# Cumulative log sums as two float32r products from the sixth unit on, with routing weights finished a step later

## The chip, the cores and the metric

The kernel runs on one core of a Trainium2 chip. A core has a matrix engine (TensorE, PE in the profile; its weight loads are listed as PEld), a vector engine (VectorE, DVE), a scalar engine (ScalarE, ACT), a general engine (GpSimd, POOL) and a sync engine (SyncE, SP) that mostly issues transfers. The engines run their own instruction streams in order and wait for each other through semaphores. Sixteen DMA engines move data between memory and the on-chip buffer. Matrix products are written to PSUM, which has eight banks here.

The metric is the time of one execution on the device in microseconds (us); lower is better. The figure used is the median over several executions.

## The reference, cut to what matters

The first half is a gated linear recurrence over 768 time steps, for 4 batches and 8 heads of width 48. The second half is a two-level mixture of experts on the 3072 resulting rows.

```python
f = 1 / (1 + exp(-f_logit))
for t in range(S):
    state = f[:, :, t, :, None] * state + outer(k[:, :, t], v[:, :, t])
    y[:, :, t] = q[:, :, t] @ state
x = y.transpose(0, 2, 1, 3).reshape(3072, 384)
g_idx = argmax(x @ w_group);  e_idx = argmax(x @ w_expert[g_idx])
weight = softmax(group)[g_idx] * softmax(expert)[e_idx]
out = weight * (relu(x @ w1[g, e]) @ w2[g, e])     # one expert of 16 for each row
```

## The kernel before

**Units.** The recurrence is computed in chunks of 128 time steps. A unit is one chunk of two batches, so there are 12 units, numbered 0 to 11 (`NU` is 12): unit 2c is the first half of the batches of chunk c, unit 2c+1 the second half. A product of gates over a chunk is an exponential of a sum of logs. So a unit's gate logits are clamped (L581, `bounded`, VectorE), turned into the negative logs nl = log(1 + exp(-f)) by an Exp and a Ln on ScalarE (L591 and L594, `gated`, 128x768 elements each), and summed along time by a product with a triangular matrix of ones (L600, tile `cs`, one 128x384 float32 product for each of the unit's two batches). Two exponentials of each sum (L601, L602) scale q and k (L620, L623, `multiplied`). Then come transposes of q and k (L634) and their copies to SBUF (L635), the scores (L659, `ap`) and their triangular mask on VectorE (L662, `am`), the state (L676 `ds` on TensorE, then L682 and L683 on VectorE, the second of which needs `decays`, a transpose of the last row of each chunk, L643 and L644), the outputs (L697 from the state, L701 from the masked scores, copied by L704), the logits of the router (L717, L722, reduced by L723) and the rows turned back and copied out (L742 to L747).

**Routing.** When both units of a chunk have their logits, `route` runs for the chunk as a generator that is advanced by one step for every `r` in the order. Its steps on VectorE are: the differences to the maximum and a first mark (L187 to L191); the choice (L194 to L198); counts on TensorE and an Exp of the differences on ScalarE (L203 to L206); the position in the expert's list (L211 to L214); row and lane indices (L220 to L226); a table entry (`head` and `val`, L230 and L233); the rows' weights (`sm` to `meta`, L236 to L244, six small instructions, after which GpSimd copies the row numbers and sends the pairs to memory, L245 and L246); and last the table product on TensorE (L251, tile `tb`, which needs `val`) and its addition to the table (L256). After chunk 3 (`CLOSE`) the counts rank the experts, the weights of the first two experts are loaded (`load_early`, L760), and their first rows are gathered from memory (`early`, L505, the gather itself L393) while the last two chunks are still in work. The gather waits for the rows, which two large transfers put into memory (L758), and for the pairs of chunk 3 (L246).

**Order.** TensorE, VectorE, ScalarE and SyncE follow the program's order, which is written out by hand (L793 to L800): a string of tokens for each iteration i. A letter names a stage and the number the unit relative to i: `l` loads, `c` clamp, `g` logs and sums, `m` multiply, `t` transposes, `b` decays, `s` scores and masks, `n` state, `w` outputs, `d` logits, `x` rows out, `r` routing, `e` early experts, `o` the two large transfers. Iterations 3 to 8 take `ODD` and `EVEN` in turn, and iterations 9 to 12 have orders of their own. In iteration i the sums of unit i+1 are taken (`g+1 g+1`), and the clamp and the logs of unit i+2 are made (`c+2`, and two times `g+2`), both after the scores of unit i.

**Experts.** After the units, 16 experts are worked off, each with two products (L439 and L460 or L475) on the rows that chose it, and the results are scattered to the output.

Of the kernel before, what the change touches and what calls it, by code (L numbers as in the profile page):

```python
# [10 lines left out]
FP32 = mybir.dt.float32  # L11
I32 = mybir.dt.int32
U32 = mybir.dt.uint32
BF16 = mybir.dt.bfloat16
AF = mybir.ActivationFunctionType
OP = mybir.AluOpType
AX = mybir.AxisListType.X
# [6 lines left out]
def kernel(  # L24
# [64 lines left out]

    tri = const([P, P], FP32, "tri")  # L90
    ident = const([P, P], FP32, "ident")
    strictb = const([P, P], BF16, "strictb")
    onesb = const([P, P], BF16, "onesb")
    halves = const([P, 2], FP32, "halves")
    make_upper_triangular(nc, tri, val=1.0, diag=True)
    make_identity(nc, ident)
    nc.vector.memset(onesb, 1.0)
    nc.vector.tensor_tensor(strictb, tri, ident, OP.subtract)


# [74 lines left out]
    def restart():  # L175
        nc.vector.tensor_copy(run, base)

    def route(c, lg, sb, tabled=True, tidy=None, counted=None, ranking=None):


        def tmp(shape, name, dtype=FP32, bufs=1):
            return sb.tile(shape, dtype, tag=name, bufs=bufs, name=name)

        SHP = (P, B * (G + 1), 4)
        L = lg.rearrange("p n (a e) -> p (n a) e", e=4)
        mx = tmp([P, B * (G + 1)], "mx")
        nc.vector.reduce_max(out=mx, in_=L, axis=AX)  # L187
        dl = tmp(list(SHP), "dl")
        nc.vector.tensor_tensor(dl, L, mx.unsqueeze(2).broadcast_to(SHP), OP.subtract)
        oh = tmp(list(SHP), "oh")  # L190
        nc.vector.scalar_tensor_tensor(out=oh, in0=dl, scalar=0.0, in1=firsts, op0=OP.is_ge, op1=OP.mult)  # L191
        yield
        best = tmp([P, B * (G + 1)], "best")
        nc.vector.reduce_max(out=best, in_=oh, axis=AX)  # L194
        nc.vector.tensor_tensor(oh, oh, best.unsqueeze(2).broadcast_to(SHP), OP.is_equal)
        ohv = oh.rearrange("p (n a) e -> p n a e", n=B)
        ohe = tmp([P, B, GE], "ohe", BF16)
        nc.vector.tensor_tensor(ohe.rearrange("p n (g e) -> p n g e", e=EG), ohv[:, :, 1:G + 1, :],  # L198
                                ohv[:, :, 0, :].unsqueeze(3).broadcast_to((P, B, G, EG)), OP.mult)
        yield  # L200

        rk = bank([P, B + 1, GE], "rk")
        nc.tensor.matmul(rk[:, 0:B, :].rearrange("p n e -> p (n e)"), lhsT=strictb, rhs=ohe.rearrange("p n e -> p (n e)"), start=True, stop=False, skip_group_check=True)  # L203
        for n in range(B):
            nc.tensor.matmul(rk[:, n + 1:, :], lhsT=onesb, rhs=ohe[:, n:n + 1, :].broadcast_to((P, B - n, GE)), start=False, stop=(n == B - 1), skip_group_check=True)
        nc.scalar.activation(dl, dl, AF.Exp)  # L206
        yield
        if tidy:
            tidy(sb)
        pick = tmp([P, B, GE], "pick")  # L210
        nc.vector.tensor_tensor(pick, rk[:, 0:B, :], run.unsqueeze(1).broadcast_to((P, B, GE)), OP.add)  # L211
        nc.vector.tensor_tensor(pick, pick, ohe, OP.mult)
        nc.vector.reduce_sum(out=keys[:, c], in_=pick, axis=AX)
        nc.vector.tensor_tensor(run, run, rk[:, B, :], OP.add)  # L214
        if counted:
            counted(sb)
        yield
        if tabled:
            at = tmp([P, B, 2], "at", I32)
            nc.vector.tensor_copy(at[:, :, 0], keys[:, c])  # L220
            nc.vector.tensor_scalar(at[:, :, 1], at[:, :, 0], 7, None, OP.logical_shift_right)
            nc.vector.tensor_scalar(at[:, :, 0], at[:, :, 0], P - 1, None, OP.bitwise_and)
            atf = tmp([P, B, 2], "atf")
            nc.vector.tensor_copy(atf, at)
            ln = tmp([P, B, P], "ln", BF16)
            nc.vector.tensor_tensor(ln, lanes.unsqueeze(1).broadcast_to((P, B, P)), atf[:, :, 0:1].broadcast_to((P, B, P)), OP.is_equal)  # L226
            yield
            BLK = (P, B, 2 * GE)
            head = tmp(list(BLK), "head")
            nc.vector.tensor_tensor(head, heads_of.rearrange("p e j -> p (e j)").unsqueeze(1).broadcast_to(BLK), atf[:, :, 1:2].broadcast_to(BLK), OP.is_equal)  # L230
            val = tmp([P, 2, B, 2 * GE], "val", BF16)
            for m in range(2):
                nc.vector.tensor_tensor(val[:, m], head, part[:, c, :, m:m + 1].broadcast_to(BLK), OP.mult)  # L233
            yield
        sm = tmp([P, B, G + 1], "sm")
        nc.vector.reduce_sum(out=sm.rearrange("p n a -> p (n a)"), in_=dl, axis=AX)  # L236
        nc.vector.tensor_scalar(sm, sm, 1e-9, None, OP.add)
        nc.vector.reciprocal(out=sm, in_=sm)
        ew = tmp([P, B, G], "ew")
        nc.vector.tensor_tensor(ew, sm[:, :, 1:G + 1], ohv[:, :, 0, :], OP.mult)  # L240
        ws = tmp([P, B], "ws")
        nc.vector.reduce_sum(out=ws, in_=ew, axis=AX)
        meta = tmp([P, B, 2], "meta", bufs=2)
        nc.vector.tensor_tensor(meta[:, :, 0], ws, sm[:, :, 0], OP.mult)  # L244
        nc.gpsimd.tensor_copy(meta[:, :, 1].bitcast(I32), token[:, c, :])  # L245
        nc.gpsimd.dma_start(out=rows_of(c)[:, :, DM:RW], in_=meta)  # L246
        yield
        if tabled:
            tb = bank([P, 2, GE, 2], "tb")
            for b in range(B):  # L250
                nc.tensor.matmul(tb.rearrange("p m e j -> p m (e j)"), lhsT=ln[:, b], rhs=val[:, :, b, :], start=(b == 0), stop=(b == B - 1))  # L251
            if ranking:
                yield
                ranking(sb)
                yield
            nc.vector.tensor_tensor(table, table, tb, OP.add)  # L256
# [262 lines left out]
    with ExitStack() as fast:  # L519
# [28 lines left out]

        CORNERS = [(b, h) for b in range(2) for h in range(2)]
        KEPT = NU - 4  # L550
        live = {}
        groups, ends = {}, {}

# [30 lines left out]
        def gated(i):  # L584
# [5 lines left out]
            for b in parts(i):  # L590
                nc.scalar.activation(nl[:, b], nl[:, b], AF.Exp, bias=0.0, scale=-1.0)  # L591
                if i:
                    yield
                nc.scalar.activation(nl[:, b], nl[:, b], AF.Ln, bias=1.0, scale=1.0)  # L594
            eq, qh, kh = pads["eq"][i % 2], w["qh"], pads["kh"][i % 3]
            w.update(eq=eq, kh=kh)
            yield
            for b in range(2):
                cs = bank([P, H, D], "cs")
                nc.tensor.matmul(cs.rearrange("t h d -> t (h d)"), lhsT=tri, rhs=nl[:, b], start=True, stop=True)  # L600
                nc.scalar.activation(eq[:, b, :, 0:D], cs, AF.Exp, bias=0.0, scale=-1.0)  # L601
                nc.scalar.activation(kh[:, b, :, 0:D], cs, AF.Exp, bias=0.0, scale=1.0)  # L602
                if b:

                    if s == 0:
                        ends[c] = sb.tile([B * HP, P], FP32, tag="ends", bufs=1, name="ends")
                    side(i).dma_start(out=ends[c][2 * HP * s:2 * HP * (s + 1), :], in_=eq[P - 1:P].rearrange("o b (a r) d -> o (b a) (r d)", r=2))  # L607
                yield
# [56 lines left out]
        def stated(i):  # L665
# [12 lines left out]
            dst = new[:, :, :, 0:D]  # L678
            gv = w["g"].unsqueeze(3).broadcast_to((P, 2, HP, D))
            if c:  # L680
                sp = sb.tile([P, 2, HP, D], FP32, tag="sp", bufs=1, name="sp")
                nc.vector.tensor_tensor(sp, old[:, :, :, 0:D], ds, OP.add)  # L682
                nc.vector.tensor_tensor(dst, sp, gv, OP.mult)  # L683
            else:
                nc.vector.tensor_tensor(dst, ds, gv, OP.mult)
            yield
# [81 lines left out]
        def routed(c):  # L768

            yield from route(c, groups[c], sb, tidy=fix_early if c == CLOSE + 1 else None, counted=load_early if c == CLOSE else None,  # L770
                             ranking=(lambda pool: ranked(GE, pool)) if c == NC - 1 else None)
            if c == CLOSE:
                choose_early(sb)
                first.append(early())
# [4 lines left out]
        def advance(gens):  # L779
            if gens and next(gens[0], True):  # L780
                gens.pop(0)

        first, routes = [], []

# [3 lines left out]
            t1 t1 t1 t1 b1 c2 g2 g2 s1 s1 s1 s1 p d0 g2 g2 n0 n1 w1 w1 m2 m2 l4 n1  # L790
            d0 x1 x1 t2 t2 t2 t2 c3 g3 g3 x1 s2 s2 s2 s2 w2 g3 g3 d1 w2 n2 m3 m3 c4 g4 g4""".split()
        BEGUN = 3
        EVEN = "l+2 d-2 n-1 r r r x-1 x-1 t t t t g+1 g+1 x-1 r s s s s c+2 w d-1 g+2 w g+2 n m+1 m+1".split()  # L793
        ODD = "l+2 d-2 r r x-1 x-1 t t t t b n-1 g+1 g+1 x-1 r s s s s c+2 w d-1 g+2 w g+2 n m+1 m+1 r n".split()
        ORDERS = {
            NU - 3: "l+2 o d-2 r r x-1 x-1 t t t t b n-1 r g+1 g+1 x-1 r s s s s c+2 w d-1 g+2 w g+2 n m+1 m+1 r n".split(),
            NU - 2: "d-2 r x-1 x-1 r t t t t r g+1 g+1 x-1 s s s s w d-1 w n m+1 m+1".split(),
            NU - 1: "d-2 r r n-1 x-1 x-1 t t t t r x-1 r s s s s w b d-1 w r r".split(),
            NU: "d-2 r e d-1 x-1 x-1 d-1 x-1 r r r e e r e r r e r r e r e r r e e e e e".split(),
# [3 lines left out]
        def step(nm, i):  # L803
# [7 lines left out]
                send_kept()  # L811
            elif nm == "h":
                next(turning)
            elif 0 <= i < NU:
                if nm == "l":

# [251 lines left out]
```

## Time and profile before

| | |
|---|---|
| median of 13 runs (lowest to highest) | 416.72 us (415.74 to 417.56) |
| the profiled execution's own time | 417.07 us |
| its span in the profile | 415.2 us |
| TensorE busy | 405.8 us, 98% of the span |
| VectorE busy | 266.9 us, 64% |
| ScalarE busy | 157.1 us, 38% |
| GpSimd busy | 83.2 us, 20% |
| granted TensorE clock | 1.00 throughout |
| mean transfer rate | 214 GB/s |

Times in the profile are counted from the start of the span. "Busy" counts instructions in flight; for TensorE the ends of matrix products are modelled, so 98% does not mean that it never waits. Starts are exact, and the best reading of how long a group takes in a full stream is the distance from its start to the next group's start. The recurrence lies in the first 135 us or so. Iterations 3 to 11 begin, counted by the router's transpose L722 on TensorE, at 37.97, 48.79, 59.25, 70.06, 80.81, 91.62, 102.08, 113.77 and 124.23 us.

### The profile page before, as it was taken

To read this page: it belongs to the slowest core of one execution; us is meant where nothing else is said; L and a number is where in the kernel's file an instruction comes from. 1 tells how busy PE (TensorE), PEld (TensorE's weight loads), DVE (VectorE), ACT (ScalarE), POOL (GpSimd) and SP (SyncE) were. 2 spreads that over 40 slices of the span, in tenths; PEclk is the share of its full clock that TensorE was granted. 3 is DMA by queue.
4 is the path that set the end of the run, shared out by engine and by line. 5 is a ranking of instruction groups with operands and counts; after the bars stand their busy time and mean duration, and the time that the engine had idled before them with its cause. 6 is when DMAs were issued, how large, how long until landed. Compare 5 with 4: busy or idle time off the path is not lost.

```text
span 415.2 us, 10066 instructions
## 1 busy us (share of the span) xinstructions
PE 405.8 (98%) x4047; PEld 374.6 (90%) x4047; DVE 266.9 (64%) x778; ACT 157.1 (38%) x353; POOL 83.2 (20%) x127
## 2 busy tenths in 40 slices
PE   8999999999998999999999999999999999999995
PEld 3888888888777978989999999999999999999992
DVE  5666887878898631640799767485595595594230
ACT  6777766666554311211223122222231231231220
POOL 4000010101012147001041221311321321120230
PEclk9999999999999999999999999999999999999999
DMA  9999997878999549985739467585595695585010
GB/s 176 211 196 217 192 171 147 153 138 155 288 335 388 197 162 340 383 290 193 271 88 335 130 250 255 169 323 187 188 351 151 236 340 182 203 321 162 28 47 24
DMA packets 132145, 88.98 MB, mean 214 GB/s; under 512 B 102582, under 2 KB 122748, under 8 KB 132090
## 3 DMA queue, kind: packets, MB, share of 16 engines
q1 hardware_dynamic: 125666, 75.50, 62.2%
q0 software_dynamic: 5792, 11.92, 9.4%
q10 hardware_dynamic: 632, 0.83, 0.6%
q8 instruction: 34, 0.56, 0.5%
q14 instruction: 21, 0.17, 0.1%
HBM read 78.71 MB, written 9.83 MB: 213 GB/s over the span
## 4 chain that ended last, share of the span: by engine, by line
PE 49%; issue 29%; DMA 9%; POOL 6%; DVE 3%; POOLq 1%; ACT 1%
PE hp L439 12%; PE yo L475 7%; DMA out_dram<-yt,xg 6%; PE ap L659 5%; PE y L701 5%; PE cs L600 4%; PE yo L460 4%; POOL out_dram L450 4%; PE x_ps L742 2%; PE tr_k L634 2%; POOL xg L393 2%; PE tr_q L634 2%; PE ds L676 2%; DMA xg<-x_dram,rows_e 2%; PE y L697 2%
## 5 line engine op out<-in xcount | busy, mean ns | idle before, releaser
L439 PE MATMUL hp<-xe,w 128*128 128x128 f32 (+14 forms) x864 | 138.6, 320 | 0.0
L439 PEld LDWEIGHTS hp<-xe,w 128*128 128x128 f32 x864 | 135.8, 191 | 0.8
L475 PE MATMUL yo<-h,w 128*128 128x230 f32 (+13 forms) x672 | 115.8, 333 | 0.0
L422 DVE STREAM_TRANSPOSE yr<-yT 32x192 f32<-32x192 f32 (+1 forms) x208 | 70.5, 339 | 70.4 <-ACT yT L476 67.8
L475 PEld LDWEIGHTS yo<-h,w 128*128 128x128 f32 x672 | 113.7, 190 | 0.2
L415 DVE STREAM_TRANSPOSE xe<-xg 32x192 f32<-32x192 f32 (+1 forms) x208 | 69.7, 335 | 8.6 <-PE hp L439 5.6
L440 ACT ACTIVATE h<-hp 128x256 f32<-128x256 f32 (+14 forms) x72 | 34.4, 478 | 103.6 <-PE hp L439 103.6
L450 POOL DMA_INDIRECT out_dram<-yt,xg x32 | 34.4, 1076 | 150.1 <-ACT yt L447 144.5
L476 ACT COPY yT<-yo 128x230 f32<-128x230 f32 (+13 forms) x42 | 13.5, 325 | 80.5 <-PE yo L475 80.5
L393 POOL DMA_INDIRECT xg<-x_dram,rows_p x30 | 29.6, 987 | 51.8 <-DMA out_dram<-yt,xg 28.7
L662 DVE TENSOR_TENSOR am<-ap,tri 128x512 f32<-128x512 f32 x48 | 29.8, 681 | 11.0 <-PE ap L659 11.0
L701 PE MATMUL y<-am,v 128*64 128x128 f32 x384 | 24.8, 276 | 0.4
L701 PEld LDWEIGHTS y<-am,v 128*64 128x64 f32 x384 | 21.1, 137 | 3.8 <-issue 2.3
L659 PE MATMUL ap<-Tq,Tk 48*64 48x128 f32 x768 | 23.8, 273 | 0.0
L659 PEld LDWEIGHTS ap<-Tq,Tk 48*64 48x64 f32 x768 | 20.8, 133 | 1.6 <-issue 1.1
L460 PE MATMUL yo<-w,h 128*128 128x384 f32 x64 | 21.3, 486 | 0.0
L600 PE MATMUL cs<-ld_f,tri 128*128 128x384 f32 x48 | 18.6, 506 | 0.1
L460 PEld LDWEIGHTS yo<-w,h 128*128 128x128 f32 x64 | 11.9, 190 | 7.4
L607 POOL DMA_DIRECT2D ends<-eq x10 | 5.4, 541 | 55.5 <-ACT eq L601 55.5
L447 ACT ACTIVATE yt<-yr,xg 128x384 f32<-128x384 f32 (+13 forms) x26 | 14.4, 604 | 5.4 <-DVE yr L422 5.4
L704 ACT COPY xT<-y 128x512 f32<-128x512 f32 x24 | 13.5, 581 | 5.0 <-PE y L701 5.0
L634 PE MATMUL tr_q<-ident,qh 128*128 128x128 f32 x96 | 14.5, 273 | 0.5 <-issue 0.4
(173 smaller groups left out, 369.2 us busy)
## 6 DMA issues: line engine op xcount, KB each, us to landing
w<-in_moe_w_dram SPq DMA_DIRECT2D x34, 1536.0 KB, 10.3
qh<-in_q_dram SPq DMA_DIRECT2D x12, 384.0 KB, 5.2
ld_k<-in_k_dram SPq DMA_DIRECT2D x12, 384.0 KB, 5.8
v<-in_v_dram SPq DMA_DIRECT2D x12, 384.0 KB, 6.0
ld_f<-in_f_logit_dram SPq DMA_DIRECT2D x11, 384.0 KB, 6.4
x_dram<-x_kept SPq DMA_DIRECT2D x2, 1536.0 KB, 11.2
x_dram<-x POOLq DMA_DIRECT2D x2, 384.0 KB, 8.1
x_dram<-x ACTq DMA_DIRECT2D x2, 384.0 KB, 8.2
```

The costliest lines, as they stand in the source:

```text
L393: nc.gpsimd.indirect_dma_start(out=w["x"][:, j, :], out_offset=None, in_=x_dram[0:1 + top, :], in_offset=bass.IndirectOffsetOnAxis(ap=rows ...
L415: squares(w, lambda n, k_, rk, g, rg: nc.vector.transpose(out=xT[rg, 0:n, k_], in_=x[rk, 0:n, g]))
L422: squares(w, lambda n, k_, rk, g, rg: nc.vector.transpose(out=y[rk, 0:n, g], in_=yT[rg, 0:n, k_]))
L439: nc.tensor.matmul(hp[:, o, :], lhsT=w1[:, ko, (f + o) * P:(f + o + 1) * P], rhs=w["xT"][:, ko, :], start=(ko == 0), stop=(ko == KO - 1))
L440: nc.scalar.activation(h[:, f:f + 2, :], hp, AF.Relu)
L450: sent = nc.gpsimd.indirect_dma_start(out=out, out_offset=bass.IndirectOffsetOnAxis(ap=w["x"][0:m, j, DM + 1:RW].bitcast(U32), axis=0), in ...
L460: nc.tensor.matmul(yp, lhsT=w["h"][:, fo, :], rhs=w2[:, fo, :], start=(fo == 0), stop=(fo == FO - 1))
L475: nc.tensor.matmul(yp, lhsT=w2[:, fo, m * P:(m + 1) * P], rhs=w["h"][:, fo, :], start=(fo == 0), stop=(fo == FO - 1))
L600: nc.tensor.matmul(cs.rearrange("t h d -> t (h d)"), lhsT=tri, rhs=nl[:, b], start=True, stop=True)
L634: nc.tensor.transpose(out=pt[:, a, :], in_=w[nm + "h"][:, b, 2 * a:2 * a + 2, :].rearrange("t r d -> t (r d)"), identity=ident)
L659: nc.tensor.matmul(ap[r][half, a, :], lhsT=w["Tk"][rows, b, a, half], rhs=w["Tq"][rows, b, a, :], start=True, stop=True)
L701: nc.tensor.matmul(ys[b][DP * h:DP * h + DP, a, :], lhsT=w["v"][:, b, 2 * a + (b ^ h), :], rhs=w["am"][b][:, b ^ h, a, :], start=(c == 0 a ...
```

## The change

Four things change.

1. From unit 5 on (`SPLIT`), the logs go to their sums as two float32r numbers. ScalarE copies the logs into a float32r tile (`most`), VectorE subtracts that from the logs into a second one (`least`), and each sum is two accumulated products with a float32r copy of the triangular matrix in place of one float32 product.
2. The clamp of unit i+2 and its Exp, Ln and copy move ahead of the scores of unit i; the subtraction comes after unit i's multiplications.
3. For chunks 0, 1 and 2 the six instructions of the rows' weights, GpSimd's copy and the transfer are put off to a new token `q` in the next odd iteration, so the route has one step less; the two tiles that they read are doubled. The two `val` instructions become one.
4. The state's addition and multiplication work in place, without the tile `sp`.

```diff
+    nc.vector.tensor_copy(trir, tri)
...
-        dl = tmp(list(SHP), "dl")
+        dl = tmp(list(SHP), "dl", bufs=2)
...
-        oh = tmp(list(SHP), "oh")
+        oh = tmp(list(SHP), "oh", bufs=2)
...
-            for m in range(2):
-                nc.vector.tensor_tensor(val[:, m], head, part[:, c, :, m:m + 1].broadcast_to(BLK), OP.mult)
+            nc.vector.tensor_tensor(val, head.unsqueeze(1).broadcast_to((P, 2, B, 2 * GE)), part[:, c].rearrange("p b m -> p m b").unsqueeze(3).broadcast_to((P, 2, B, 2 * GE)), OP.mult)
...
+        def weights_of_rows():
...
+        if late is not None:
+            late.append(weights_of_rows)
+        else:
+            weights_of_rows()
+            yield
...
+            pieces = [nl]
+            if i >= SPLIT:
+
+                pieces = [sb.tile([P, 2, H * D], F32R, tag=nm, bufs=1, name=nm) for nm in ("most", "least")]
+                nc.scalar.copy(pieces[0], nl)
+                yield
+                nc.vector.tensor_tensor(pieces[1], nl, pieces[0].bitcast(FP32), OP.subtract)
...
-                nc.tensor.matmul(cs.rearrange("t h d -> t (h d)"), lhsT=tri, rhs=nl[:, b], start=True, stop=True)
+                for n, piece in enumerate(pieces):
+                    nc.tensor.matmul(cs.rearrange("t h d -> t (h d)"), lhsT=trir if i >= SPLIT else tri, rhs=piece[:, b], start=(n == 0), stop=(n == len(pieces) - 1))
...
-                sp = sb.tile([P, 2, HP, D], FP32, tag="sp", bufs=1, name="sp")
-                nc.vector.tensor_tensor(sp, old[:, :, :, 0:D], ds, OP.add)
-                nc.vector.tensor_tensor(dst, sp, gv, OP.mult)
+                nc.vector.tensor_tensor(dst, old[:, :, :, 0:D], ds, OP.add)
+                nc.vector.tensor_tensor(dst, dst, gv, OP.mult)
...
-        EVEN = "l+2 d-2 n-1 r r r x-1 x-1 t t t t g+1 g+1 x-1 r s s s s c+2 w d-1 g+2 w g+2 n m+1 m+1".split()
-        ODD = "l+2 d-2 r r x-1 x-1 t t t t b n-1 g+1 g+1 x-1 r s s s s c+2 w d-1 g+2 w g+2 n m+1 m+1 r n".split()
+        EVEN = "l+2 d-2 n-1 r r x-1 x-1 t t t t c+2 g+1 g+1 x-1 r g+2 g+2 s s s s w d-1 w n m+1 m+1 g+2".split()
+        ODD = "l+2 d-2 r r q x-1 x-1 t t t t b n-1 c+2 g+1 g+1 x-1 r g+2 g+2 s s s s w d-1 w n m+1 m+1 g+2 r n".split()
...
-            NU - 3: "l+2 o d-2 r r x-1 x-1 t t t t b n-1 r g+1 g+1 x-1 r s s s s c+2 w d-1 g+2 w g+2 n m+1 m+1 r n".split(),
+            NU - 3: "l+2 o d-2 r r q x-1 x-1 t t t t b n-1 c+2 r g+1 g+1 x-1 r g+2 g+2 s s s s w d-1 w n m+1 m+1 g+2 r n".split(),
...
+            elif nm == "q":
+                for close in closings:
+                    close()
+                closings.clear()
```

## The prediction

> **What bounds the kernel now.** I read the chain that ended last in order of time first, because it says which engine sets the pace in each stage. Its middle part (start, length, what):
>
> ```profile
> 94.57 1.29 PE cs L600 x4
> 95.86 0.12 PE tb L251 x4
> 95.98 1.91 PE ap L659 x64
> ...
> 112.23 0.87 DVE qh L620
> 113.10 0.87 DVE kh L623
> 113.97 0.09 DVE at L220
> ...
> 117.38 0.29 PE tb L251 x4
> ...
> 127.93 7.01 DMA xg<-x_dram,rows_e
> 134.93 0.14 issue
> 135.07 0.52 PE xg_ps L429 x3
> ```
>
> Up to iteration 9 (start 102.1) the chain is TensorE alone, and the sums `cs` take 1.29 us of each iteration in four records. In iterations 9 and 10 it is VectorE, from the masks to `val`, and then the gather of the early rows. After 139 us it is TensorE again, in the experts, which the change doesn't touch.
>
> Next I read VectorE and TensorE in order of time around iterations 7 and 8 (start, length, engine, line; in brackets idle time and its releaser):
>
> ```profile
> 82.96 0.55 DVE L682 TENSOR_TENSOR sp<-st,ds 128x384 f32<-128x384 f32 x1
> 84.66 0.56 DVE L683 TENSOR_TENSOR st<-sp,decays 128x384 f32<-128x384 f32 x1 [1.15 <-ACT decays L644]
> 86.59 2.48 DVE L662 TENSOR_TENSOR am<-ap,tri 128x512 f32<-128x512 f32 x4 [1.38 <-PE ap L659]
> 88.99 0.55 DVE L581 TENSOR_SCALAR ld_f<-ld_f 128x768 f32<-128x768 f32 x1
> 89.46 0.95 DVE L620 TENSOR_TENSOR qh<-qh,eq 128x768 f32<-128x768 f32 x1
> 90.33 0.95 DVE L623 SCALAR_TENSOR_TENSOR kh<-kh,ld_k 128x768 f32<-128x768 f32 x1
> 91.19 0.21 DVE L211 TENSOR_TENSOR pick<-rk,run 128x64 f32<-128x64 f32 x1
> 94.86 0.49 DVE L233 TENSOR_TENSOR val<-head,part 128x128 bf16<-128x128 f32 x2
> 95.27 0.23 DVE L236 TENSOR_REDUCE sm<-dl 128x20 f32<-128x80 f32 x1
> 96.61 0.21 DVE L256 TENSOR_TENSOR table<-table,tb 128x64 f32<-128x64 f32 x1
> ```
>
> ```profile
> 85.45 1.98 PE L659 MATMUL ap<-Tq,Tk 48*64 48x128 f32 x64
> 95.70 0.28 PE L251 MATMUL tb<-val,ln 128*128 128x64 bf16 x4
> ```
>
> VectorE has no idle time between the masks of an odd iteration (86.59) and the end of `val` (94.86 + 0.49 = 95.35), and TensorE asks for `val` at 95.70: a margin of 0.35 us. The same margin stands in iterations 3 to 4 and 5 to 6. So TensorE sets the pace, and VectorE is close behind it in every second iteration. In iterations 9 and 10, where the ranking's instructions come on top, VectorE is the bound.
>
> **The change part by part.**
>
> *Sums.* Taken away for units 5 to 11: a product of 1.29 us a unit. In its place four products of 384 columns with float32r operands, which no row shows. Bounds: the table product `tb` in bf16 takes 0.12 us for four times 64 columns, 0.47 ns a column, so 0.18 us for 384 and 0.72 us a unit. The transposes, float32 in one record, take 0.44 us for four times 128 columns, 0.33 us for 384 and 1.31 us a unit, no gain. If each float32r product costs what a float32 one does, it is 2.58 us a unit. I take 0.72: a float32 product here is two records of 0.84 ns a column each (1.29 / 4 / 384), together 3.6 times the bf16 row, which reads as a number multiplied in parts; a number rounded to fit once is nearest to the bf16 row. Gain 0.57 us a unit.
>
> The Trainium skill (FP8 and Floating Point Precision, TensorE Precision Notes) gives true FP32 four passes and a reduced FP32 one truncated read; by that two rounded products cost half, 0.65 us a unit, and the sum below would be 0.2 us lower. No run here shows it yet.
>
> *Rounding on ScalarE.* One copy of 128x768 a unit, not shown: 0.75 us by the Exp of that shape (89.57 to the next start at 90.32), 0.72 to 0.75 by scaling the 128x512 copies (0.48 from start to start). ScalarE idles 2.36 us before `lgT` in iterations 5 and 7, where Exp, Ln and copy, 2.25 us, go now. In iteration 7 they end near 88.7, 0.4 us after TensorE has `lT` ready (88.87 - 0.57); `lgT` is read by L722 some 2 us later. Cost 0; with that cover gone, 0.4 us an iteration.
>
> *Rest on VectorE.* One subtraction of 128x768 a unit, not shown. Below: the clamp of that shape, 0.47 us from start to start (88.99 to 89.46). Above: a mask, 0.60 for 512, so 0.90, or 1.02 by its length of 0.68. Nearest is `qh`, also two tensors in SBUF: 0.87. It stands after `kh`, before the routing that ends in `val`.
>
> *Clamp ahead.* 0.47 us leaves the stretch after the masks and falls between `st` and the masks, where VectorE idles 1.38 us. The load that it needs is issued an iteration earlier (94.35 for unit 11) and lands in 6.4 us. SyncE's loads keep their order.
>
> *`val` in one.* Two instructions, 0.49 us; one of 256 elements is 0.42 us by `less` (128x256). Gain 0.07.
>
> *Rows' weights later.* Six instructions, 1.29 us (73.71 to 74.99), leave the even iteration after `val`, where only the table's addition follows them, and land before `sp` in iterations 5, 7 and 9. There `st` waits 1.15 us for the decays, so `st` moves by 0.17 us only. The scores wait for `sp`, whose bank they take over: 82.96 + 1.29 + 0.55 = 84.80, against scores at 85.45 - 0.57 = 84.88; it just fits. Then `st` and the clamp end at 85.8, masks are due at 86.0. On GpSimd the copy (0.20) and transfer (0.79) of the pairs move along: the `ends` transfer that stood behind them in even iterations comes earlier, and in iteration 9 the rows of unit 8 (104.15) go out some 1.5 us later, read only by the gathers after 149 us.
>
> *The rest.* The state in place: two instructions as before, 0. `trir`: one copy in a 0.70 us wait of VectorE at 1.69 us, 0; uncovered 0.3. Doubled small tiles: 0.
>
> **The sum.** Odd iterations 5 and 7: 0.57 each, -1.14. Even iterations 4, 6 and 8: `val` moves by +0.87 - 0.47 - 0.07 = 0.33 against the masks, to 95.68, and is seen 0.06 later (117.32 to 117.38 in iteration 10), so `tb` stands at 95.74 whatever the sums take, and the 0.57 turns into a wait of TensorE for `val`, with the next scores and all else of TensorE queued behind it: +0.04 each, +0.12. So iteration 9 begins 1.02 us early. From there VectorE is the chain: +0.17 at `st`, +0.87 for the subtraction, -0.07, the clamp moves within it: +0.97 to `val` and to chunk 3's pairs (118.67). Unit 11's sums save 0.57 behind that, but TensorE waits for the gather (1.43 us at 135.07), which waits for those pairs: 0. Sum: -1.02 + 0.97 = -0.05 us, on the profiled execution's 417.07 (span 415.2) 417.0; that stood 0.35 above the median 416.72, so 416.7. A change under 0.2%, 0.83 us, is about what a measurement can't tell from none.
>
> **The rivals.**
> 1. *Faster: the subtraction runs at the clamp's 0.47.* Then `val` keeps its margin: 0.40 more in each of iterations 4, 6 and 8, and 0.40 less in iteration 9: -0.05 - 1.6 = -1.65, 415.1. For it: the clamp shows that VectorE can pass 768 float32 in 0.47. Against: every two-tensor row takes 0.87. A smaller part of it comes from sums at less than 0.18 a product. It counts from 0.2 us less on the subtraction.
> 2. *Slower: float32r streams at the pace of the transposes.* Then no iteration gains, even ones lose 0.04, and iterations 9 and 10 pay 0.97 in full: +1.1, 417.8. For it: both are four-byte operands in one record. It decides from 0.29 us a product upward, where the odd iterations give back less than 0.26; at 0.25 they would give 0.58.
> 3. *Much slower: float32r costs what float32 does.* 1.29 more in each of iterations 4 to 8, 6.45, and 0.97 after: +7.4, 424.1. For it only that the operand is as wide.
>
> The gather, 7.01 us on DMA engines that are full from 105 to 140 us, can land some tenths off either way.
>
> **How the numbers follow.** Forecast 0.46; rival 1 0.28; rival 2 0.16; rival 3 0.06; 0.04 for a gather or a wait that is late by more than 0.83. So faster 0.28, same 0.46, slower 0.26. Time 416.7, with 416.0 to 417.4 for the likeliest case alone. The range reaches over rivals 1 and 2, 415.0 to 418.0, and leaves out rival 3, the late gather and what of rival 1 lies deeper.
>
> **What would show it.** Right: the `cs` products of a unit within some 0.7 us; odd iterations (L722 to L722) 10.2 us against 10.8; even ones unchanged at 10.5 to 10.8, with a wait at `tb` released by `val`; iteration 9 at 101.1; the gather at 127.9. Wrong: `cs` at 1.3 us or more, even iterations that shorten too, a subtraction under 0.7, or scores that wait for `sp`.

## The result, and the profile after

The changed kernel took 422.03 us (median of 7 runs, 421.75 to 423.29) against 416.72 us (median of 31 runs, 415.48 to 417.56) on the same chip. The ratio is 1.0137, 95% interval 1.0125 to 1.0149. The forecast was 416.7 us, no change that can be told, with a range of 415.0 to 418.0; the kernel is 5.3 us slower. Its profiled execution took 421.48 us with a span of 419.6 us, against 417.07 and 415.2.

The products did what was forecast. The first view is that of the tile `cs` on TensorE (engine, operation, number: shortest, median and longest duration in ns, first and last start in us), of after:

```profile
L619 PE MATMUL cs<-ld_f,tri x20: 486/486/978, 5.6 to 43.8; 128*128 128x384 f32 x20
L619 PE MATMUL cs<-most,trir x14: 336/379/445, 57.8 to 124.5; 128*128 128x384 f32 x14
L619 PE MATMUL cs<-least,trir x14: 332/336/338, 58.1 to 124.7; 128*128 128x384 f32 x14
```

A float32r product is one record, where a float32 one is two; the four products of a unit take 0.70 us in the chain (below), the float32 ones took 1.29. But iterations 3 to 9 now begin at 39.66, 55.12, 65.03, 75.27, 86.31, 96.55 and 107.21 us, in place of 37.97, 48.79, 59.25, 70.06, 80.81, 91.62 and 102.08. So 1.7 us are lost before iteration 3, and iteration 3 itself takes 15.46 us instead of 10.82; it sums only unit 4, which isn't split. The chain that ended last shows what came in there (start, length, what):

```profile
32.70 7.00 DMA ld_f<-in_f_logit_dram
...
41.58 7.24 DMA ld_f<-in_f_logit_dram
48.82 0.02 issue
48.84 0.04 DVE ld_f L592
...
49.92 0.69 DVE am L681
50.61 0.04 issue
50.65 3.22 PE y L719 x29
...
58.06 0.70 PE cs L619 x4
58.76 0.17 PE tb L261 x4
```

VectorE in order of time says the same (start, length, line; in brackets the idle time before it and what ended it):

```profile
44.90 0.56 DVE L701 TENSOR_TENSOR st<-st,decays 128x384 f32<-128x384 f32 x1 [2.38 <-ACT decays L663]
48.84 0.56 DVE L592 TENSOR_SCALAR ld_f<-ld_f 128x768 f32<-128x768 f32 x1 [3.38 <-DMA ld_f<-in_f_logit_dram]
49.32 2.48 DVE L681 TENSOR_TENSOR am<-ap,tri 128x512 f32<-128x512 f32 x4
```

The clamp of unit 5 waits 3.38 us for its load, and the masks, due earlier, stand behind it in VectorE's order. TensorE has nothing to do for 2.5 us and then runs at half its clock: the `y` products are granted 0.50 from 51 to 54 us, and 29 of them take 3.22 us where 32 took 1.90 before. Two windows of after show it (start and end, length, PE busy, clock, share of the DMA engines, GB/s):

```profile
49.00:50.00 1.00, 0.00 (x0) 1.00 0.93 127
51.00:52.00 1.00, 1.00 (x13) 0.50 1.27 179
```

The loads are late because all of them have become slower. Busy time by windows (start and end, length, then PE, PEld, DVE, ACT, POOL busy, clock, share of the DMA engines, GB/s), first of before, then of after:

```profile
0.00:45.00 45.00, 43.34 (x683) 33.23 (x687) 28.60 (x76) 33.09 (x69) 6.77 (x44) 1.00 1.06 199
```

```profile
0.00:45.00 45.00, 42.34 (x619) 31.70 (x623) 27.46 (x74) 31.81 (x65) 5.88 (x42) 1.00 1.22 170
45.00:60.00 15.00, 12.51 (x233) 11.57 (x229) 10.50 (x26) 9.50 (x22) 0.52 (x1) 0.89 1.22 172
```

The DMA engines are busier and move less, and the whole kernel still moves 88.98 MB in 132,145 packets, as before. The page's list of transfers gives the median from issue to landing, last column, of after:

```profile
qh<-in_q_dram SPq DMA_DIRECT2D x12, 384.0 KB, 7.2
ld_k<-in_k_dram SPq DMA_DIRECT2D x12, 384.0 KB, 6.8
v<-in_v_dram SPq DMA_DIRECT2D x12, 384.0 KB, 7.3
ld_f<-in_f_logit_dram SPq DMA_DIRECT2D x11, 384.0 KB, 7.0
```

Before, these were 5.2, 5.8, 6.0 and 6.4. They are also issued later: up to this point SyncE issues one load after another without a pause, and each takes longer to issue (`ld_f` 2.03 us against 1.67, medians). The load of unit 5's logits, of before and then of after (start, length of issuing):

```profile
36.03 1.47 SPq L575 DMA_DIRECT2D ld_f<-in_f_logit_dram  x1
```

```profile
41.58 2.03 SPq L586 DMA_DIRECT2D ld_f<-in_f_logit_dram  x1
```

So this load is issued 5.55 us later, and it then takes 7.24 us to land, where the loads of `ld_f` took 5.7 to 6.6 before. Nothing in the change touches a load's source, size or queue. What moved is where the loads write: the change's tiles (512 bytes a partition for `trir`, 6144 for `most` and `least`, 640 for the doubled small tiles, 1536 less without `sp`) push the kept tiles, among them the targets of q and v, up by 5760 bytes, which is 22.5 times 256. In the compiled kernels the first of them begins at byte 163,072 of each partition before, a multiple of 256, and at 168,832 after, 128 above one. A row of a head is 48 numbers, 192 bytes, written at steps of 256 bytes. Before, each piece lay in one 256-byte line; after, each lies across two.

The gather follows the late iterations. Of after, the chain again:

```profile
132.51 7.04 DMA xg<-x_dram,rows_e
139.55 0.14 issue
139.68 0.52 PE xg_ps L439 x3
```

The experts begin at 139.68 instead of 135.07, 4.6 us later, and that is what the end shows.

### The profile page after: what moved, and what is told of

The parts are those of the page before. It is cut to its first block, busy times and chain, and to the rows that moved or that the text cites. A ratio compares the mean times of both kernels' runs of the same rounds, so it can differ in the third digit from the quotient of the medians.

```text
span 419.6 us, 10075 instructions
## 1 busy us (share of the span) xinstructions
PE 404.7 (96%) x4047; PEld 376.1 (90%) x4047; DVE 273.3 (65%) x780; ACT 164.0 (39%) x360; POOL 83.2 (20%) x127
## 2 busy tenths in 40 slices
DMA packets 132145, 88.98 MB, mean 212 GB/s; under 512 B 102582, under 2 KB 122748, under 8 KB 132090
## 4 chain that ended last, share of the span: by engine, by line
PE 34%; issue 30%; DMA 14%; DVE 10%; POOL 6%; SPq 2%; ACT 2%; POOLq 1%; DVEq 0%
PE hp L449 12%; PE yo L485 6%; DMA out_dram<-yt,xg 6%; PE yo L470 4%; POOL out_dram L460 4%; DMA ld_f<-in_f_logit_dram 3%; PE y L719 3%; SPq L586 2%; POOL xg L403 2%; PE ap L678 2%; DMA ld_k<-in_k_dram 2%; DMA xg<-x_dram,rows_e 2%; DVE am L681 2%; PE ds L695 1%; DMA ends<-eq 1%
## 5 line engine op out<-in xcount | busy, mean ns | idle before, releaser
L719 PE MATMUL y<-am,v 128*64 128x128 f32 x384 | 26.4, 286 | 4.5 <-DVE am L681 4.2
L719 PEld LDWEIGHTS y<-am,v 128*64 128x64 f32 x384 | 22.6, 142 | 8.1 <-DVE am L681 6.3
L653 PE MATMUL tr_k<-ident,kh 128*128 128x128 f32 x96 | 14.4, 274 | 0.9 <-DVE kh L642 0.9
## 6 DMA issues: line engine op xcount, KB each, us to landing
w<-in_moe_w_dram SPq DMA_DIRECT2D x34, 1536.0 KB, 10.5
```

The source lines that it names most:

```text
L653: nc.tensor.transpose(out=pt[:, a, :], in_=w[nm + "h"][:, b, 2 * a:2 * a + 2, :].rearrange("t r d -> t (r d)"), identity=ident)
L719: nc.tensor.matmul(ys[b][DP * h:DP * h + DP, a, :], lhsT=w["v"][:, b, 2 * a + (b ^ h), :], rhs=w["am"][b][:, b ^ h, a, :], start=(c == 0 a ...
```

## The experiments

Each group was measured beside the kernel before on the same chip, and the ratios are to that. Six chips took part; the starts of iterations agree between them (the kernel before at a good place takes 63.82 us for iterations 3 to 8 in e3 and 63.96 in e11), so these are compared across chips too. On two of them the kernel before takes 416.4 to 416.7 us, on four 421.4 to 422.2; the last section says where those differ.

**Is it the place of the tiles or the order of the work?** Four kernels, one chip.

```diff
+        nc.gpsimd.memset(kept([P, 96], "spacer"), 0.0)   # e1, in the changed kernel: tiles at 0 of 256
+        nc.gpsimd.memset(kept([P, 32], "spacer"), 0.0)   # e2, in the kernel before: at 128 of 256
+        nc.gpsimd.memset(kept([P, 16], "spacer"), 0.0)   # e3, in the kernel before: at 64 of 256
         pads = {}
```

```diff
 # e4: as e1, and
-        SPLIT = 5
+        SPLIT = NU
 # and the third g+2 (copy and subtraction) out of the orders
```

> The changed kernel with an unused tile of 384 bytes a partition ahead of the kept tiles (v, q, k, exponentials, states), so that these begin at a multiple of 256 bytes again, as before the change; every instruction of the units is the same. Theory A (place): the new tiles pushed the kept tiles to 128 bytes past a multiple of 256, the loads of q and v write pieces of 192 bytes every 256 bytes, each piece then straddles a multiple of 256, and these writes slow all loads. It expects the loads to land in 5 to 6.5 us again (7.0 to 7.3 in the changed kernel), VectorE's wait of 3.4 us for the logits at 48.8 us gone, and 416.2 to 417.2 us in all, which is the forecast without the slow loads. Theory B (order): the clamp now stands where its load has not landed; it expects the wait and 421 to 422 us to stay.

> The kernel before with an unused tile of 128 bytes a partition ahead of the kept tiles, which puts them 128 bytes past a multiple of 256. Nothing else. Theory A: loads of q and v at 7 us or more, a rate near 170 GB/s instead of 199 in the first 45 us, and 3 to 6 us slower (420 to 423); a little less than in the changed kernel, because the clamp comes later here. Theory B: 416.7 within 0.8.

> The kernel before with an unused tile of 64 bytes ahead of the kept tiles, which puts them 64 bytes past a multiple of 256: a piece of 192 bytes then ends on the next multiple of 256 and straddles none. Theory A with straddling as the cause: 416.7 within 0.8. Theory A with any place off a multiple of 128 or 256 as the cause: slower by 3 us or more. Theory B: 416.7 within 0.8.

> The changed kernel with the kept tiles at a multiple of 256 again and without the split: float32 sums as before, no copy and no subtraction, but the new order of clamp and logs, the rows' weights a step later, one val instruction, and the state in place. The forecast's working gives the new order alone nothing (-0.2 to +0.2 us, 416.5 to 416.9), and the split on top of it -0.1 to -0.2, so within 0.8 us of e1. If the sums' gain of 0.57 us a unit reached the end, e4 would be 1.5 to 3 us slower than e1.

| kernel | ratio to the kernel before | 95% interval | GB/s, first 45 us |
|---|---|---|---|
| e1, changed, tiles at 0 | 0.9988 | 0.9964 to 1.0012 | 199 |
| e2, before, tiles at 128 | 1.0103 | 1.0061 to 1.0145 | 171 |
| e3, before, tiles at 64 | 0.9996 | 0.9970 to 1.0021 | 201 |
| e4, changed, tiles at 0, no split | 0.9996 | 0.9972 to 1.0019 | 198 |

A spacer of 384 bytes a partition, which computes nothing, takes the whole loss away, and one of 128 bytes makes the kernel before slow. The place is what the loss needs; it costs the kernel before 1.0% (e2; 0.5% in the one execution of e10 below) and the changed one 1.4%. What follows the place is the rate, not every landing time: in e1 `v` took 8.1 us to land, and in e2 `qh` 5.8. With the tiles back the change is worth nothing that can be told, as was forecast, and so is the split on top of the new order (e1 against e4).

**Which places are bad?** The same spacer in the kernel before with 192 and with 32 bytes, one execution of each, on a chip like the first.

> The kernel before with 192 bytes put ahead of the kept tiles, so that each 192-byte piece of q and v lies at 192 to 384 of a 256-byte raster. Theory S (a piece that crosses a multiple of 256 bytes is slow to write): as with 128 bytes, 165 to 178 GB/s in the first 45 us at a share above 1.15, and a span some 4 us above that of the kernel before. Theory H (only a start at half of the raster, 128, is bad): as the kernel before, 195 to 203 GB/s, the same span.

> The kernel before with 32 bytes put ahead of the kept tiles: pieces at 32 to 224 of the 256-byte raster, no longer at a multiple of 64 bytes, but crossing no multiple of 256. Theory S: as the kernel before, 195 to 203 GB/s in the first 45 us. Theory H': the start has to be a multiple of 64 bytes: 165 to 185 GB/s, and a later end.

The window of the first 45 us, of e10 and then of e11:

```profile
0.00:45.00 45.00, 41.33 (x619) 31.45 (x623) 27.42 (x73) 31.85 (x66) 6.05 (x43) 1.00 1.20 171
```

```profile
0.00:45.00 45.00, 43.14 (x683) 33.32 (x687) 28.65 (x76) 33.08 (x69) 6.80 (x45) 1.00 1.06 199
```

At 192 the pieces cross a multiple of 256 and are slow: span 416.8 us, one time of 418.70 against 416.42. At 32, no multiple of 64, they cross nothing and are fast: span 414.4, 416.31. So 0, 32 and 64 are good, 128 and 192 bad, as theory S has it; the loss in e10 is 2.4 us of span against e11, where some 4 were expected. A start in the upper half of the raster would fit the five places as well as crossing does; a place that tells the two apart, 96 for one, was not run. The Trainium skill (DMA: Bandwidth & Descriptors, How a descriptor splits into AXI transactions) says of reads that a bus transaction of a transfer must start from a 256-byte-aligned address, and its table counts one transaction more for a 576-byte descriptor that begins at 224 than for one that begins at 0. The five places, all of them writes, agree with it. The targets of f and k, which have no gaps (steps of 192 bytes), cross in most rows too and yet landed in 5.8 and 6.4 us in the kernel before; no run here explains why these are spared.

**Is crossing nothing enough in the changed kernel?** e12 puts 192 bytes ahead of its tiles, to 64 of 256.

> The changed kernel with 192 bytes ahead of its kept tiles, so that they begin at 64 of a 256-byte raster: pieces at 64 to 256, which cross nothing. Theory S (crossing a multiple of 256 is what cost the 5.3 us): loads as in the kernel before, 195 to 203 GB/s in the first 45 us, iterations 10.2 (odd, 5 and 7) and 10.4 to 10.5 (even), and a ratio of 0.998 to 1.002, as in the first experiment. Rival (the place of 0 mod 256 was needed, or the first experiment's chip hid a loss): ratio above 1.004.

Ratio 0.9980 (0.9961 to 0.9999), 199 GB/s. It is.

**How much do the slow loads take by themselves?** In the kernel before at a bad place (e10) iteration 3 still takes 10.82 us: its clamp is behind the masks, and waits 0.78 us for its load there. So I put the changed kernel's clamp, and with it the logs and the copy, back there in iteration 3 alone, the tiles still at 128 (e14), with the changed kernel itself on the same chip (e15).

```diff
+            3: "l+2 d-2 r r q x-1 x-1 t t t t b n-1 g+1 g+1 x-1 r s s s s c+2 w d-1 g+2 w g+2 n m+1 m+1 g+2 r n".split(),
```

> The changed kernel, its tiles still at 128 of 256 (slow loads), with the clamp of unit 5 back behind the masks in iteration 3 and nowhere else. Theory W (the clamp's wait of 3.38 us for its load stood ahead of the masks, TensorE waited 2.5 us for them and then ran at half clock): iteration 3 takes some 11 us instead of 15.5 and the experts begin 2 to 4 us earlier than in the changed kernel; the ratio to the kernel before falls from 1.014 to between 1.004 and 1.009. Rival L (the loads are late by the same amount wherever the wait stands: what iteration 3 gains, iteration 4 loses): within 0.7 us of the changed kernel.

> The changed kernel as it is, beside the run before it on the same chip. Both theories: slower than the kernel before, ratio 1.011 to 1.017, iteration 3 about 15.5 us.

e14: 1.0181 (1.0149 to 1.0214); e15: 1.0127 (1.0099 to 1.0156). Iteration 3 fell from 15.46 to 10.82 us, and iteration 4 rose from 9.93 to 14.49. VectorE in order of time, of e14, and the chain of e14 in iteration 4:

```profile
50.58 0.55 DVE L592 TENSOR_SCALAR ld_f<-ld_f 128x768 f32<-128x768 f32 x1
...
54.63 0.96 DVE L612 TENSOR_TENSOR least<-ld_f,most 128x768 fp32r<-128x768 f32 x1 [1.77 <-ACT most L610]
```

```profile
52.99 0.75 ACT ld_f L605
...
53.77 0.84 ACT most L610
...
54.63 0.96 DVE least L612
...
59.18 0.44 DVE val L235
...
59.66 0.28 PE tb L261 x4
59.93 3.00 PE ap L678 x64
62.93 1.45 PE y L715 x32
```

Here the clamp no longer waits for its load. VectorE stands 1.77 us at the subtraction instead, because the logs and the copy went behind the masks with the clamp; the routing, `val` and `tb` stand behind it, TensorE waits 2.8 us at `tb`, and then the scores and the first outputs run at half clock (3.00 and 1.45 us instead of 1.91 and 0.87). So neither theory holds as it stands. Theory W was right that the clamp's place makes iteration 3 long, and wrong that putting it back would win time. Rival L has the sum of both iterations right, 25.31 us against 25.39, but not for its reason: the loss in iteration 4 is a new wait on VectorE and ScalarE, not the late load, and e14 as a whole is 2.1 us slower than e15, where 0.7 at most was expected. With the split, unit 5's gates have to be through clamp, logs, copy and subtraction before VectorE gets to iteration 4's routing, so the order that hides the late load in the kernel before only moved the wait here. That e14 is slower as a whole comes from its first 40 us (iteration 3 begins 2.35 us later, mean clock 0.92 in the first 45 us against 1.00); why, these runs don't say. How much of the 5.3 us is the place and how much the order is known only from the kernel before (e2, e10); the new order without the split at a bad place was not run.

**Does the wait at `tb` eat the gain of the sums, as the prediction had it?** Four kernels with the tiles at 0, on a chip that takes 422.24 us for the kernel before. e5 issues `tb` after the first scores in even iterations; e6 also reorders iterations 9 and 10 and leaves unit 11 unsplit; e7 is e6 without the split; e8 is e1 without the subtraction and its two products (its sums lack what the rounding cuts off).

```diff
 # e5
-        EVEN = "... c+2 g+1 g+1 x-1 r g+2 g+2 s s s s w ..."
+        EVEN = "... c+2 g+1 g+1 x-1 g+2 g+2 s r s s s w ..."
 # e6, as well: iteration 9, and iteration 10 with tb after the first scores
-            NU - 3: "l+2 o d-2 r r q x-1 x-1 t t t t b n-1 c+2 r g+1 g+1 x-1 r g+2 g+2 s s s s w d-1 w n m+1 m+1 g+2 r n"
+            NU - 3: "l+2 o d-2 r r x-1 x-1 t t r t t b r n-1 c+2 g+1 g+1 x-1 g+2 g+2 s s s s w d-1 w n m+1 m+1 r n q"
```

> The changed kernel with its tiles moved back (as in the first experiment), and in even iterations the routing step that issues tb now stands after the first scores instead of ahead of them. Theory V (the prediction's step: in even iterations the subtraction delays val, and TensorE stands at tb with the scores behind it, so the sums' 0.57 us turns into a wait): the wait of some 0.43 us at tb goes in iterations 4, 6 and 8, these take about 10.0 us instead of 10.4 to 10.5, iteration 9 begins 1.3 us earlier than in the first experiment, and the time is about 1.3 us below that kernel's, a ratio to the kernel before of 0.995 to 0.997. Theory T (something else, loads or ScalarE, paces the even iterations, and tb's wait only stands in front of it): no difference to the first experiment, ratio 0.998 to 1.000.

> As the run before it, and iteration 9 reordered too: the rows' weights go from ahead of the ranking to the end of the iteration, the clamp and the state go behind the ranking, rk is issued among the transposes; unit 11 keeps its plain float32 sum (no subtraction ahead of val in iteration 10); in iteration 10 tb stands after the first scores. Theory V: the chain on VectorE in iteration 9 gets shorter, TensorE no longer waits 1.5 us for the masks there, and the half clock that followed that wait in the first experiment (3.79 us for products that take 1.90) is gone: the experts begin 1.6 to 1.9 us earlier than in the first experiment, ratio 0.993 to 0.996, faster than the kernel before. Theory T: the experts begin when the gather or the loads let them, ratio 0.998 to 1.000.

> The order of the run before it, but no unit is split: float32 sums everywhere, no rounding, no subtraction (SPLIT = NU). Theory V: in this order TensorE is the pace of iterations 4 to 8 and the split is worth its 0.57 us in each: this kernel is 2.5 to 3 us slower than the run before it, ratio 0.999 to 1.003. Theory T: the split is worth nothing in any order, ratio within 0.002 of the run before it.

> The changed kernel with its tiles moved back and its own order, the subtraction and its two products left out: the sums of units 5 to 11 take the rounded number alone. Theory V: the subtraction is what delays val: odd iterations 9.8 us, even ones 10.0, iteration 9 begins some 2 us earlier than in the first experiment, ratio 0.993 to 0.996. Theory T: VectorE's 0.87 us is not what holds the even iterations; they stay at 10.4 to 10.5, ratio 0.998 to 1.000.

Starts of iterations in the table are those of `lg` on TensorE; the experts begin with the first `xg_ps`. The first two rows are from the first group's chip, where the kernel before takes 421.47 us; the kernel before stands there as e3.

| kernel | iterations 3 to 8, us | iteration 9, us | experts begin, from iteration 3's start | ratio (95%) |
|---|---|---|---|---|
| before at 64 (e3) | 63.82 | 11.69 | 96.0 | 0.9996 (0.9970 to 1.0021) |
| e1 | 62.97 | 13.85 | 95.7 | 0.9988 (0.9964 to 1.0012) |
| e5 | 61.68 | 12.78 | 94.5 | 0.9942 (0.9920 to 0.9965) |
| e6 | 61.68 | 11.58 | 94.0 | 0.9944 (0.9923 to 0.9965) |
| e7 | 64.62 | 11.59 | 97.0 | 1.0003 (0.9985 to 1.0021) |
| e8 | 60.41 | 13.84 | 92.7 | 0.9900 (0.9879 to 0.9922) |

The wait was real and could be had: moving `tb` takes 1.29 us off iterations 3 to 8, and e5 is 0.6% faster than the kernel before. In this order the split is worth 2.94 us of iterations 3 to 8 (e6 against e7), 0.59 for each of iterations 4 to 8; in the change's own order it was 0.85 us (e1 against e4, 63.82), of which nothing could be told at the end. Part of the 2.94 is that the new place of `tb` doesn't suit the unsplit kernel: e7 is 0.80 us slower there than e4, with even iterations of 10.72 to 10.73 us. Against the best order that was run without the split, the two together are worth 2.14. The subtraction is what held the even iterations up, as far as e8 can say, which leaves out two products as well: even and odd iterations alike take 9.9 us; the even ones lose 0.6 to 0.7, of which the products explain the 0.34 that the odd ones lose. In e6 iteration 9 gets 1.2 us shorter, yet the end is that of e5; its experts begin 0.6 us earlier, and TensorE stands as much longer in the second expert's products, here in the chain of e6:

```profile
159.95 1.47 PE hp L449 x13
161.42 1.53 issue
...
163.34 1.03 issue
...
165.09 12.37 PE hp L449 x56
```

That this is the wait for the next weights is argued, not shown: every profile from a chip at 421 us and more has it, and none of the five from the two chips at some 416.5 (before, after, e9, e10, e11).

e13 repeats e5 with the tiles at 64, on another chip.

> As the run before it, with tb after the first scores in even iterations. Theory V, on a chip whose kernel before takes 421 us or more: as the fifth experiment, ratio 0.992 to 0.997. On one whose kernel before takes some 416.5 us the rows' pairs of chunk 3 are ready 1.3 us earlier than in the run before it, and the gather with them: ratio 0.996 to 0.998. Rival G (there the gather lands when the DMA engines let it, some 135 us, whatever TensorE does): ratio 0.999 to 1.002.

Ratio 0.9961 (0.9943 to 0.9979), on a chip at 422.08 us. Theory V holds there too; whether the gain is the same where the gather decides, as on the first chip, stays open, since no run of this order fell on one.

**The subtraction on GpSimd.** e9 is e6 with all of units 5 to 11 split and the subtraction moved.

```diff
-                nc.vector.tensor_tensor(pieces[1], nl, pieces[0].bitcast(FP32), OP.subtract)
+                nc.gpsimd.tensor_tensor(pieces[1], nl, pieces[0].bitcast(FP32), OP.subtract)
```

> The reordered kernel (tiles moved back, tb after the first scores, iteration 9 reordered), with all of units 5 to 11 split and the subtraction issued on GpSimd, in the scores' time, instead of on VectorE. No row shows such a subtraction on GpSimd; its writes of 128x384 zeros take 0.43 us, so two reads and a write of 128x768 may take 0.9 to some 3 us, and the next sums stand 5 us behind. Theory V: VectorE loses 0.87 us an iteration, the qh and kh products and the routing end earlier; in the order used here TensorE is already the pace of iterations 4 to 8, so the gain shows in iterations 9 and 10 only: 0 to 1 us below the reordered kernel, ratio 0.991 to 0.995. Rival G (GpSimd is too slow, or slows VectorE's instructions beside it): the sums wait for the rest, ratio above 0.997.

On a chip at 416.42 us it took 1.0020 (1.0010 to 1.0030): rival G. e6 was not run on such a chip, so the ratio can't be set against its 0.9944; but iterations 3 to 8 take 62.97 us in e9 and 61.68 in e6, and that loss comes with the move. GpSimd and VectorE in order of time, of e9:

```profile
98.60 2.35 POOL L613 TENSOR_TENSOR least<-ld_f,most 128x768 fp32r<-128x768 f32 x1 [2.20 <-ACT most L611]
```

```profile
98.30 0.95 DVE L640 TENSOR_TENSOR qh<-qh,eq 128x768 f32<-128x768 f32 x1
99.16 2.60 DVE L643 SCALAR_TENSOR_TENSOR kh<-kh,ld_k 128x768 f32<-128x768 f32 x1
101.69 0.23 DVE L742 TENSOR_REDUCE lgs<-lg 128x40 f32<-128x80 f32 x1
```

The subtraction takes 2.35 us on GpSimd, and `kh`, 0.95 us elsewhere, takes 2.60 beside it and ends some 0.8 us after it: VectorE lost 1.65 us to save 0.87; six of these `kh` rows read 2.58 to 2.61. The Trainium skill (SBUF — State Buffer, SBUF: two separate sides) calls the pair of ports that the two share an exclusive lock, held for the whole instruction by the one that starts first, while the other blocks; this takes a VectorE instruction with two inputs in SBUF and a GpSimd one that reads SBUF, as here. The rows agree: `kh` starts 0.56 us after the subtraction and ends 0.81 us after its end.

## Why the prediction was wrong

**What failed.** Two steps. The first is "Doubled small tiles: 0" and the copies and tiles beside it: they were costed by the instructions that use them, and nothing was asked about where they push other tiles. The runs show that this place is worth the whole loss (ratios of 1.0137 and, on another chip, 1.0127 with it, 0.9988 and 0.9980 without). The second is *Clamp ahead*: "the load that it needs is issued an iteration earlier (94.35 for unit 11) and lands in 6.4 us". That took unit 11's margin for unit 5's, and a duration of before for after. Unit 11's load is issued 7.7 us before iteration 9 begins; unit 5's, the first that the split needs, was issued at 36.03 in the kernel before, only 1.9 us before iteration 3. With the slow loads (the first 45 us move 170 GB/s instead of 199) it is issued at 41.58 and lands 7.24 us later, so that the clamp waits with the masks behind it. Iteration 3 starts 1.7 us late and takes 4.6 us more; by iteration 4 the kernel is 6.33 us late. Iterations 4 to 8 give back 1.20 (from 55.12 to 107.21 they take 52.09 us, against 53.29), iterations 9 to 11 and the gather 0.5, and 4.6 are left at the experts. "A load that is late" stood in no rival: the largest one, 424.1, was to come from the products.

**What the case without that cost shows.** e1 and e12 are the change as the prediction priced it, step by step:
- *Sums.* 0.72 us a unit was forecast; 0.70 was measured, above the 0.65 that the prediction gives beside it. Rivals 2 and 3, and with them every slow float32r, are out.
- *Rest on VectorE.* 0.87 from start to start forecast and measured (74.45 to 75.32 in after), so rival 1, 0.47, is out as well. The copy took 0.73 us from start to start (51.19 to 51.92 in after), where 0.75 was taken.
- *Odd iterations 5 and 7.* 10.2 us forecast, 10.24 in e1.
- *Even iterations.* "Unchanged at 10.5 to 10.8, with a wait at `tb` released by `val`": 10.50, 10.50 and 10.67. The chain of e1 in iteration 8, where VectorE hands over to TensorE only at `val`:

```profile
89.75 0.87 DVE least L613
...
94.20 0.44 DVE val L235
94.64 0.04 issue
94.68 0.28 PE tb L261 x4
94.95 1.91 PE ap L679 x64
```

- *Iteration 9* at 101.1 forecast, 101.06 in e1; against e3 on the same chip iterations 3 to 8 are 0.85 us shorter, where 1.02 was forecast.
- *Iterations 9 and 10.* +0.97 forecast; 11.69 and 10.46 before, 12.79 and 10.21 in e12, +0.85. In e1 the same wait had a consequence that the prediction lacked, the half clock:

```profile
109.38 0.68 DVE am L682
110.06 0.04 issue
110.10 3.79 PE y L720 x31
```

Iteration 9 took 13.85 us there, and iteration 10, 9.14 instead of 10.21, made up for it: in e12 TensorE waits for `val` in iteration 10, and in e1 it gets there after `val` is done.
- *Sum.* From iteration 3 to the experts 0.3 us less than e3 on the same chip; -0.05 was forecast. The last step of the sum, that TensorE waits for the gather there and the gather for chunk 3's pairs, is not tested by it: in e1 and e12 the rows are there when TensorE asks for them.

So the forecast of no change was right for the instructions up to the experts, and wrong for the kernel, by a term that it set at nothing.

## What to carry to other kernels

Before a new tile is costed at nothing, work out which tiles it moves in the buffer, and whether targets of transfers in short pieces (192 bytes here) come to lie across multiples of 256; a spacer ahead of them is a cheap test and was a cure here. A product made faster is worth little while its engine stands at a result of another engine: look for what else can be issued ahead of that wait. Here the split alone took 0.85 us off iterations 3 to 8 and nothing that can be told off the end, the other place of `tb` without the split cost 0.80 there, and both together took off 2.14, with 0.6% at the end. The margin of a load must be read for the first unit that uses it, not for one in the steady part. A price in the trace of before holds only as long as what surrounds it stays, and a wait that is put ahead of other work on an in-order engine must be priced with its cover gone.

## What the runs showed of the hardware

- **Transfers to SBUF.** Pieces of 192 bytes at steps of 256 were slow at 128 and 192 of a 256-byte raster (169 to 171 GB/s in the first 45 us) and fast at 0, 32 and 64 (197 to 201).
- **float32r.** A product of 384 columns is one record of 0.34 us, and four of them take 0.70 us in a full stream; the float32 product of that shape is two records of 0.49, and the four records of two products take 1.29.
- **The clock.** After TensorE had idled 2.5 us (after, 47.7 to 50.2 us) and 1.6 us (e1, 108.5 to 110.1) the profile shows a granted clock of 0.50 for some 3.4 us (50.94 to 54.35 and 110.19 to 113.60, estimated from windows of 0.2 us), in which products take twice their time. In e12 1.7 us of idle time at the same place, in two waits of which the longest was 1.5, passed without it, and so did the wait of 1.43 us for the gather in the kernel before; whether the length or the moment decides, these runs don't say.
- **Chips.** The kernel before took 416.4 to 416.7 us on two chips and 421.4 to 422.2 on four. On the four, TensorE stands still in pieces in the second expert's products (2.2 us in all between 162 and 170 us in e3), and in ten of twelve profiles it falls to half clock after it, though not in e3 and e4; on the two it does neither. Small gains ahead of that point can vanish or grow there, which is why ratios are to the kernel before on the same chip.
